# Zero products at the start on TensorE, and the mask products of an attention stage on four 64x64 tiles

## The chip, the core and the metric

The kernel runs on one core of a Trainium2 chip. The metric is device microseconds of one execution, as the median of several runs. TensorE multiplies; its results land in banks of PSUM. VectorE, ScalarE and GpSimd do the rest on data in SBUF, which has 128 partitions. SyncE issues all the transfers from and to HBM. The profile calls the engines PE (PEld for its weight loads), DVE, ACT, POOL and SP; "PEq" and the like are an engine's sequencer, which waits and issues.

## The reference, cut to what matters

Attention with a local window and block summaries, then two dense blocks. Only the attention's scores matter here:

```python
def _attn_ref(q, k, v):                       # (2, 8, 768, 64) each
    block, window = (32, 16)
    k_sum = k.reshape(B, H, nb, block, D).max(axis=3)
    scores_l = scale * np.matmul(q, k.transpose(0, 1, 3, 2))
    mask_l = np.abs(pos[:, None] - pos[None, :]) < window
    scores_s = scale * np.einsum('bhsd,bhnd->bhsn', q, k_sum) + np.log(block)
    scores_l_m = np.where(mask_l, scores_l, -1000000000.0)
    a = softmax(concatenate([scores_l_m, scores_s], axis=-1))
    return a @ concatenate([v, v_sum])
...
x = mish(attn_out @ w_in) @ w_out             # first dense block, _moe_ref
out = _moe2_ref(x, phi, w1, w2)               # softmax routing to 8 experts
```

## The kernel before

All work is cut into tasks. Each names its engine, the tasks that it needs and the buffers that it takes. `Plan.run` issues them in the order of a written table, `ORDER`, and takes buffers by another, `SLOT`; so each engine's instructions stand in a fixed order, and an engine works through them strictly one behind the other.

The tokens are taken in 12 tiles of 128, t = 0 to 11. For a tile, the scores of 8 heads lie in two banks, one for each parity r of the head, 4 heads to a bank, 120 columns to a head: 96 for the window of keys, 24 for the block summaries. The 128 tokens are two halves w of 64, and each half has its own window. A score product is a 64x64 product for one head and one half (line 419); it stands on the quarter of TensorE's array given by r (rows) and w (columns). Sixteen of them make a tile, in the order head pair, r, w.

For tiles t = 0 to 4 the mask is added by TensorE. Before the score products of a tile, mask products (line 414) fill both banks: `spread_sb` (128x128) against `mask_sb` (three patterns of 128 partitions by 120 columns). Partitions 0 to 63 of the mask hold 0 or a large negative number for the 96 window columns; partitions 64 to 66 hold the logarithm of the block size, in three pieces, for the 24 summary columns. One product of 128x128 and 480 columns fills a bank; at a tile on the edge of a sequence (t = 0) it is two, of 64 columns of weights each, since the halves differ. From t = 5 VectorE adds the mask; it takes `near` and `edge_t`, which the same kind of product makes once each (lines 384 and 393).

Around the start the work is this. SP issues in this order: the keys of batch 0 (`kb`, twice), `spread`, `masks`, the queries of tile 0, two small constants, the values (`vn`, twice), the queries of tile 1, the first half of the first weight block of `w_in` (`wi`), the queries of tile 2 (which must wait until the score products of tile 0 have read their buffer), the next two halves of `wi`, and so on. VectorE reduces the keys to block summaries (line 319), and POOL places these beside the window (line 372, `kplace`, once for each half). Then come the score products of tile 0, VectorE's row maxima (427), POOL's negation (431) and ScalarE's exponentials (441).

At the same time the weights of the first dense block are made. They arrive packed, 1 MB to a load, into three staging buffers, and each load is decoded by three instructions: ScalarE (line 487), VectorE's shift (488) and VectorE's merge (489). The merge sets the staging buffer free, and SP, which waits for that, issues the next load into it. Products of the first dense block (lines 611, and 617 to 619) follow.

Of the kernel before, what the change touches and what calls it, by code (L numbers as in the profile page):

```python
# [11 lines left out]
BF16 = mybir.dt.bfloat16  # L12
# [6 lines left out]
B, H, S, D = 2, 8, 768, 64  # L19
# [4 lines left out]
KW = 120  # L24
# [69 lines left out]
]  # L94
# [81 lines left out]
def local_summary_attention_mish_soft_moe(ctx: ExitStack, tc, qh, kh, vh, kb, vn, wi, wo, phi, w1, w2a, w2b,  # L176
# [72 lines left out]
    add = pl.add  # L249
# [19 lines left out]
    def const_fill(e):  # L269
        pool.memset(bnd, TINY)  # L270
        pool.memset(bnd[:, 0:5], TINY2)
# [808 lines left out]
```

## Time and profile before

| | us |
|---|---|
| median of 3 runs (range) | 290.82 (290.64 to 290.93) |
| the profiled execution | 289.33 |
| its span, first to last instruction | 287.5 |
| PE busy in the span | 268.0 (93%), 3144 matmuls |
| ACT, DVE, POOL busy | 207.8, 195.0, 52.2 |
[...]

The profiled execution has 1.8 us outside the span and is 1.5 us below the median of the runs. PE is busy for most of the span, but the share is a mean over stages. The chain that ended last runs through DVE, ACT and transfers up to 70 us, then for long stretches through PE, and through the transfers of the last weights from 246 to 273 us.

### The profile page before, as it was taken

The numbers are of one execution on the slowest core, as the hardware profiler recorded it, in microseconds if no ns is written. First come the engines' busy times: TensorE is split into PE (matmuls) and PEld (weight loads), VectorE is DVE, ScalarE is ACT, GpSimd is POOL, SyncE is SP. The second block draws the span as 40 slices with busy tenths as digits, with TensorE's granted clock in tenths as the row PEclk, the third lists the DMA queues.
The fourth block names the chain that finished last, engine by engine and source line by source line (L and its number), as shares of the span: only waits on it lengthen the run. The fifth ranks groups of instructions, "written<-read, shape, count | busy, mean of one in ns | idle before, by whom it ended". The sixth has DMA issues, their size and how long they took to land.

```text
span 287.5 us, 7828 instructions
## 1 busy us (share of the span) xinstructions
PE 268.0 (93%) x3144; PEld 151.4 (53%) x3144; DVE 195.0 (68%) x460; ACT 207.8 (72%) x488; POOL 52.2 (18%) x91
## 2 busy tenths in 40 slices
PE   0889879999999999999999999999999998999997
PEld 0557445555456564565556545455645743234475
DVE  2489899999999898778659667686523575002352
ACT  1297889979988879999969999899459653003232
POOL 1559225430070531001211111000000010100000
PEclk9997999999999999999999999999999999999999
DMA  7999999599999879999695677989988999999997
GB/s 253 415 358 344 358 339 365 137 335 308 317 246 315 154 107 222 205 241 223 241 192 128 76 222 141 299 157 210 325 317 313 370 388 314 412 423 421 423 346 252
DMA packets 58467, 80.58 MB, mean 280 GB/s; under 512 B 44352, under 2 KB 47936, under 8 KB 53824
## 3 DMA queue, kind: packets, MB, share of 16 engines
q1 hardware_dynamic: 58432, 80.10, 91.3%
q8 instruction: 24, 0.39, 0.5%
q14 instruction: 11, 0.09, 0.1%
HBM read 66.46 MB, written 3.15 MB: 242 GB/s over the span
## 4 chain that ended last, share of the span: by engine, by line
PE 44%; DVE 20%; DMA 16%; ACT 14%; issue 5%; POOL 1%; SPq 0%; DVEq 0%; ACTq 0%; POOLq 0%
PE bank L617 8%; PE bank L619 7%; PE bank L618 7%; DMA slot<-w2b 6%; DVE slot L489 4%; ACT slot L441 4%; DMA slot<-w2a 3%; PE bank L754 2%; ACT slot L625 2%; DMA slot<-kb 2%; DMA slot<-wi 2%; PE bank L472 2%; DVE slot L488 2%; DMA slot<-wo 2%; ACT L625 2%
## 5 line engine op out<-in xcount | busy, mean ns | idle before, releaser
L617 PE MATMUL bank<-slot,slot 128*128 128x512 f16 x176 | 66.9, 380 | 0.7 <-ACT slot L625 0.7
L618 PE MATMUL bank<-slot,slot 128*128 128x512 f16 x176 | 66.7, 379 | 0.0
L619 PE MATMUL bank<-slot,slot 128*128 128x512 f16 x176 | 66.7, 379 | 0.0
L456 POOL TENSOR_TENSOR slot<-slot,sm 128x480 f32<-128x480 f32 x19 | 22.7, 1197 | 91.7 <-DVE sm L452 25.2
L625 ACT ACTIVATE slot<-bank,scal 128x512 f32<-128x512 f32 x44 | 29.2, 687 | 9.8 <-PE bank L619 6.7
L641 DVE SCALAR_TENSOR_TENSOR slot<-slot,sc,slot 128x512 f16<-128x512 f32 x40 | 30.6, 774 | 4.3 <-ACT slot L637 4.0
L619 PEld LDWEIGHTS <-slot 128*128 128x128 f16 x176 | 17.2, 98 | 21.0 <-DVE slot L480 0.3
L255 ACT COPY slot<-bank 120x512 f32<-120x512 f32 (+5 forms) x45 | 17.7, 430 | 14.3 <-PE bank L923 8.3
L617 PEld LDWEIGHTS <-slot 128*128 128x128 f16 x176 | 17.4, 99 | 16.8 <-issue 0.6
L625 ACT ACT_TABLE_LOAD x20 | 25.7, 1283 | 0.8 <-PE bank L619 0.4
L618 PEld LDWEIGHTS <-slot 128*128 128x128 f16 x176 | 17.2, 98 | 16.6 <-issue 1.5
L441 ACT ACTIVATE slot<-slot,sm 128x120 f32<-128x120 f32 x56 | 21.3, 383 | 0.6 <-DVE sm L435 0.5
L441 ACT ACTIVATE slot<-bank,sm 128x120 f32<-128x120 f32 x40 | 13.9, 369 | 10.5 <-POOL sm L431 10.5
L257 DVE COPY slot<-bank 128x256 f32<-128x256 f32 (+3 forms) x30 | 14.4, 513 | 9.8 <-PE bank L462 4.0
L489 DVE SCALAR_TENSOR_TENSOR slot<-slot,slot 128x1024 int32<-128x1024 int32 x16 | 20.4, 1277 | 0.3
L487 ACT ACTIVATE slot<-slot 128x1024 f32<-128x1024 f32 x16 | 18.6, 1172 | 1.8 <-DMA slot<-wi 1.4
L462 PE MATMUL bank<-ident_sb,slot 128*120 128x128 f32 x96 | 14.7, 278 | 2.1 <-POOL slot L456 1.3
L360 POOL COPY slot<-slot 128x192 f32<-128x192 f32 x26 | 13.8, 550 | 12.4 <-DMA slot<-kb 12.3
L967 PE MATMUL bank<-slot,slot 128*32 128x384 f32 (+1 forms) x256 | 15.2, 382 | 0.2 <-DMA slot<-w2b 0.2
L611 PE MATMUL bank<-slot,slot 128*128 128x512 f32 x32 | 15.4, 599 | 0.0
L472 PE MATMUL bank<-slot,slot 120*64 120x64 f32 x384 | 14.6, 233 | 0.5 <-ACT phi_sb L385 0.3
L419 PE MATMUL bank<-slot,slot 64*64 64x120 f32 x384 | 14.2, 289 | 0.6 <-POOL slot L372 0.6
(175 smaller groups left out, 478.4 us busy)
## 6 DMA issues: line engine op xcount, KB each, us to landing
slot<-w SPq DMA_DIRECT2D x16, 1024.0 KB, 5.5
slot<-w2a SPq DMA_DIRECT2D x12, 960.0 KB, 9.0
slot<-wi SPq DMA_DIRECT2D x8, 1024.0 KB, 6.8
slot<-wo SPq DMA_DIRECT2D x8, 1024.0 KB, 6.0
slot<-vh SPq DMA_DIRECT2D x12, 384.0 KB, 5.3
slot<-w2b SPq DMA_DIRECT2D x4, 1024.0 KB, 18.6
slot<-kb SPq DMA_DIRECT2D x4, 768.0 KB, 5.5
slot<-qh SPq DMA_DIRECT2D x12, 256.0 KB, 5.4
```

What stands on the lines that cost most here:

```text
L255: sca.copy(dst, src)
L441: sca.activation(A_b[ha.slot][:, hp], src, AF.Exp, bias=m[:, hp:hp + 1], scale=1.0 if late else 0.125, accum_out=m[:, 4 + hp:5 + hp])
L456: (pool if e == "POOL" else vec).tensor_tensor(A_b[ha.slot], A_b[ha.slot], sm_t[hq.slot][:, 4:8].unsqueeze(2).to_broadcast([128, 4, KW]), ...
L472: pe.matmul(banks[hm.slot][64 * r:64 * r + 64, 128 * hp + 64 * w:128 * hp + 64 * w + 64], Vb[i][:, w, c:c + 64], AT_b[hat2[r].slot][0:KW, ...
L487: d = add("ACT", ("dec_a%d" % n,) + name, lambda e: sca.activation(dst(), st(1).bitcast(F32), AF.Prelu, scale=2.0 ** -112, alpha=-(2.0 ** ...
L489: return add("DVE", ("dec_o%d" % n,) + name, lambda e: vec.scalar_tensor_tensor(di(), st(0), 29, di(), op0=ALU.logical_shift_right, op1=AL ...
L611: pe.matmul(banks[hb.slot], xf_b(hx.slot)[:, dc], slots[hw.slot][:, 512 * dc:512 * dc + 512], start=(dc == 0), stop=(dc == 3))
L617: pe.matmul(ps, x[:, 0, dc], w[:, 0, dc], start=(dc == 0), stop=False)
L618: pe.matmul(ps, x[:, 0, dc], w[:, 1, dc], start=False, stop=False)
L619: pe.matmul(ps, x[:, 1, dc], w[:, 0, dc], start=False, stop=(dc == 3))
L625: g_done[t, fb] = [add("ACT", ("mish", t, fb), lambda e, dst=dst, hb=hb, sc=sc: sca.activation(dst(), banks[hb.slot], AF.Mish, scale=sc), ...
L641: d = add("DVE", ("glo", t, fb), lambda e: vec.scalar_tensor_tensor(pv(1), g(), sfb[:, t // TB:t // TB + 1], pv(0), op0=ALU.mult, op1=ALU. ...
```

## The change

The order of the tasks that both kernels have, and what each engine issues of them, is the same; the tables have other numbers because 24 tasks are put in, and some buffers of equal kind (banks, small tiles) are swapped. What is new: POOL fills `vsum` with zeros first of all; TensorE runs 22 products on these zeros, 128x128 by 480 columns, into bank 0, which nobody reads; ScalarE copies halves of `spread_sb` and `mask_sb` to the other half of the partitions when they have landed; and each mask product becomes two for each quarter of the array, 96 columns a head from the window's mask and 24 from the summaries' constant.

```diff
 ORDER = [
-    6, 7, 213, 11, 22, 189, 8, 12, 2, 192, 190, 3, 188, 191, 23, 25, 194, 195, 196, 197, 214, 0, 1, 215, 9, 10,
+    7, 8, 9, 10, 11, 12, 13, 14, 15, 16, 17, 18, 19, 20, 21, 22, 23, 24, 25, 26, 27, 28, 29, 31, 32, 2, 3, 4, 212,
...
+    def both_halves(e):
+        lo, hi = HALF
+        sca.copy(spread_sb[hi, 0:64], spread_sb[lo, 0:64])
+        sca.copy(spread_sb[lo, 64:128], spread_sb[hi, 64:128])
+        sca.copy(mask_sb[hi, :, 0:96], mask_sb[lo, :, 0:96])
+        sca.copy(mask_sb[lo, 0, 96:KW], mask_sb[hi, 0, 96:KW])
+    L_mask, L_spread = add("ACT", ("mask2",), both_halves, [L_spread, L_mask]), None
+
+    def add_mask(ps, r, w, of, stop):
+
+        a, at = ps.shape[1], (64 * r, 64 * w)
+        for stat, row, cols in ((slice(0, 64), of, slice(0, 96)), (slice(64, 128), 0, slice(96, KW))):
+            mov = mask_sb[HALF[r], row, cols]
+            pe.matmul(ps[HALF[w], :, cols], spread_sb[HALF[r], stat], mov.unsqueeze(1).to_broadcast([64, a, cols.stop - cols.start]), start=cols.start == 0, stop=stop and cols.start > 0, tile_position=at)
...
+    Z_w = add("POOL", ("fillw",), lambda e: pool.memset(vsum, 0.0))
+    hwarm = Hold(hring)
+    zeros = vsum.bitcast(BF16)
+    warm = [Z_w]
+    for j in range(22):
+        warm.append(add("PE", ("warm", j), lambda e: pe.matmul(banks[hwarm.slot][:, 0:480], zeros[:, 0:128], zeros[:, 0:480], start=True, stop=True), [warm[-1]], acq=[] if j else [hwarm], use=[hwarm] if j else []))
...
-        vc = add("ACT", ("vgather", b), gather, [vs] + old_v, use=[hb])
+        vc = add("ACT", ("vgather", b), gather, [vs] + (old_v or [warm[-1]]), use=[hb])
...
-                for rows, of in () if late else [(slice(0, 128), 1)] if kind == 1 else [(slice(0, 64), min(kind, 1)), (slice(64, 128), max(kind, 1))]:
-                    pe.matmul(ps[rows], spread_sb[:, rows], mask_sb[:, of].unsqueeze(1).to_broadcast([128, 4, KW]), start=True, stop=False)
+                for w, of in () if late else [(0, min(kind, 1)), (1, max(kind, 1))]:
+                    add_mask(ps, r, w, of, False)
```

`near_mask` and `edge_mask` call `add_mask` too, for r = 0 and both halves.

TensorE's rows at the start of the program before: the mask products of tile 0 are its first, and its score products follow.

```order
L1076 UNCONDITIONAL_BRANCH
L414 LDWEIGHTS spread_sb
L414 MATMUL bank_64<-mask_sb,spread_sb 64x480
...
L414 LDWEIGHTS spread_sb
L414 MATMUL bank_65<-mask_sb,spread_sb 64x480
L419 MATMUL bank_64<-slot_90,slot_88 64x120 x2
L419 MATMUL bank_65<-slot_90,slot_88 64x120 x2
```

The same place of the changed program, from the last of the 22 zero products on (line 292).

```order
L292 LDWEIGHTS vsum
L292 MATMUL bank_61<-vsum 128x480
L280 LDWEIGHTS spread_sb
L280 MATMUL bank_64<-mask_sb,spread_sb 64x4x96
L280 LDWEIGHTS spread_sb
L280 MATMUL bank_64<-mask_sb,spread_sb 64x4x24
...
L280 LDWEIGHTS spread_sb
L280 MATMUL bank_65<-mask_sb,spread_sb 64x4x24
L443 MATMUL bank_64<-slot_90,slot_88 64x120 x2
L443 MATMUL bank_65<-slot_90,slot_88 64x120 x2
```

The zero products stand ahead of everything, and for a tile there are eight mask products in pairs, a wide and a narrow one on each quarter of the array, before the score products (line 443 now).

ScalarE's rows at the start of the program before: after loading its table it goes straight to the exponentials of tile 0, then to the first decoding step.

```order
L1007 ACT_TABLE_LOAD
L441 ACTIVATE slot_91,sm_106<-bank_64,sm_106 128x120 x4
L395 ACTIVATE edge_t<-bank_67 128x240
L441 ACTIVATE slot_91,sm_107<-bank_65,sm_107 128x120 x4
L487 ACTIVATE slot_77<-slot_80 128x1024
L255 COPY vsum<-bank_68 24x128 x4
```

And of the changed program.

```order
L1031 ACT_TABLE_LOAD
L269 COPY spread_sb<-spread_sb 64x64
L270 COPY spread_sb<-spread_sb 64x64
L271 COPY mask_sb<-mask_sb 64x3x96
L272 COPY mask_sb<-mask_sb 64x24
L465 ACTIVATE slot_91,sm_106<-bank_64,sm_106 128x120 x4
L419 ACTIVATE edge_t<-bank_67 128x240
L465 ACTIVATE slot_91,sm_107<-bank_65,sm_107 128x120 x4
L511 ACTIVATE slot_77<-slot_80 128x1024
```

Four copies are put in between the table load and the exponentials; behind them ScalarE's order is the old one.

## Rows read from the trace of the kernel before

**Rows 1.** Chain of waits, 0 to 70 us: start us, us, what.
```profile
1.21 6.03 DMA slot<-kb
7.26 1.76 DVE slot L319
...
24.52 5.99 DMA slot<-wi
...
61.84 5.41 DMA slot<-wo
```

**Rows 2.** Timeline of PE: start us, us, engine, line, operation, shapes, count [idle before].
```profile
7.79 1.01 PE L414 MATMUL bank<-mask_sb,spread_sb 128*64 128x480 bf16 x4 [7.79 <-DMA mask_sb<-masks]
9.39 2.08 PE L419 MATMUL bank<-slot,slot 64*64 64x120 f32 x32 [0.59 <-POOL slot L372]
11.41 0.41 PE L393 MATMUL bank<-mask_sb,spread_sb 128*64 128x120 bf16 x4
11.75 2.77 PE L328 MATMUL bank<-slot,bmean_sb 128*24 128x128 f32 x48
14.45 0.58 PE L414 MATMUL bank<-mask_sb,spread_sb 128*128 128x480 bf16 x2
14.96 1.05 PE L419 MATMUL bank<-slot,slot 64*64 64x120 f32 x32
...
20.90 1.63 PE L419 MATMUL bank<-slot,slot 64*64 64x120 f32 x32
...
25.84 1.88 PE L611 MATMUL bank<-slot,slot 128*128 128x512 f32 x4
```

**Rows 3.** Windows of one us: PE, PEld, DVE, ACT, POOL busy, PEclk, DMA share, GB/s.
```profile
9.00:10.00 1.00, 0.60 (x9) 0.61 (x13) 0.01 (x1) 0.00 (x0) 0.48 (x2) 1.00 1.01 412
...
22.00:23.00 1.00, 1.00 (x22) 0.70 (x16) 0.96 (x2) 0.96 (x6) 0.88 (x1) 0.50 0.94 328
```

**Rows 4.** Timeline of ACT, 11 to 25 us.
```profile
15.13 0.40 ACT L441 ACTIVATE slot<-bank,sm 128x120 f32<-128x120 f32 x1
...
15.84 1.16 ACT L487 ACTIVATE slot<-slot 128x1024 f32<-128x1024 f32 x1 [0.22 <-DMA slot<-wi]
17.02 1.06 ACT L255 COPY vsum<-bank 24x128 f32<-24x128 f32 x4
18.11 0.59 ACT L255 COPY slot<-bank 120x512 f32<-120x512 f32 x1
...
20.41 1.18 ACT L487 ACTIVATE slot<-slot 128x1024 f32<-128x1024 f32 x1
```

**Rows 5.** Timeline of DVE, 9 to 25 us.
```profile
16.16 0.82 DVE L456 TENSOR_TENSOR slot<-slot,sm 128x480 f32<-128x480 f32 x1
16.90 0.64 DVE L427 TENSOR_REDUCE sm<-bank 128x4 f32<-128x480 f32 x1
17.58 0.17 DVE L431 TENSOR_SCALAR sm<-sm 128x4 f32<-128x4 f32 x1
17.66 0.69 DVE L488 TENSOR_SCALAR slot<-slot 128x1024 int32<-128x1024 int32 x1
...
19.71 1.31 DVE L489 SCALAR_TENSOR_TENSOR slot<-slot,slot 128x1024 int32<-128x1024 int32 x1
...
21.86 0.66 DVE L488 TENSOR_SCALAR slot<-slot 128x1024 int32<-128x1024 int32 x1
22.56 1.89 DVE L489 SCALAR_TENSOR_TENSOR slot<-slot,slot 128x1024 int32<-128x1024 int32 x1
```

**Rows 6.** Timeline of POOL, 0 to 15 us.
```profile
0.73 0.13 POOL L270 MEMSET bnd<- 128x35 f32 x1 [0.29 <-POOLq L1073]
...
5.59 0.18 POOL L343 MEMSET slot<- 128x96 f32 x1
...
9.07 0.48 POOL L372 COPY slot<-slot 128x96 f32<-128x96 f32 x2 [0.76 <-DVE slot L319]
```

**Rows 7.** Timeline of SP's issues, 7 to 12 us.
```profile
11.92 0.43 SPq L496 DMA_DIRECT2D slot<-wi  x1
```

**Rows 8.** DMA issues at 1.67, 11.92 and 21.09 us: KB each, us to landing.
```profile
spread_sb<-spread SPq DMA_DIRECT2D x1, 32.0 KB, 5.8
...
slot<-wi SPq DMA_DIRECT2D x1, 1024.0 KB, 8.4
...
slot<-wi SPq DMA_DIRECT2D x1, 1024.0 KB, 5.7
```

**Rows 9.** Windows by stage, columns as in rows 3.
```profile
2.00:15.00 13.00, 6.62 (x94) 4.37 (x94) 5.14 (x6) 2.50 (x15) 5.06 (x20) 1.00 1.00 382
...
25.00:27.00 2.00, 2.00 (x17) 1.41 (x15) 1.95 (x5) 1.91 (x4) 1.97 (x4) 1.00 0.91 250
27.00:53.00 26.00, 23.04 (x172) 12.54 (x171) 24.74 (x50) 23.26 (x49) 11.41 (x13) 1.00 0.99 346
```

More of the change, by code (lines that the diff above doesn't have):

```diff
@@ L96 @@
     "DVE": [
[4 rows of a table removed]
[4 rows of a table added]
     ],
     "POOL": [
-        196, 199, 203, 222, 229, 243, 246, 250, 253, 267, 270, 274, 277, 291, 294, 298, 301, 317, 323, 366,
-        388, 407, 413, 426, 432, 445, 451,
+        220, 223, 227, 246, 253, 267, 270, 274, 277, 291, 294, 298, 301, 315, 318, 322, 325, 341, 347, 390,
+        412, 431, 437, 450, 456, 469, 475,
     ],
@@ L383, in near_mask, with mm @@
         hm = Hold(mring)
-        q = add("PE", ("near_mm",), lambda e: pe.matmul(banks[hm.slot][:, 0:KW], spread_sb, mask_sb[:, 1], start=True, stop=True), [L_spread, L_mask] + W2_parts, acq=[hm])
+        def mm(e):
+            for w in range(2):
+                add_mask(banks[hm.slot][:, 0:KW].rearrange("p (a k) -> p a k", a=1), 0, w, 1, True)
+        q = add("PE", ("near_m4",), mm, [L_spread, L_mask] + W2_parts, acq=[hm])
         near_done.append(add("ACT", ("near_ev",), lambda e: sca.mul(near, banks[hm.slot][:, 0:KW], 0.125), [q], use=[hm]))
@@ L391, in mm @@
             for n in range(2):
-                for rows, of in ((slice(0, 64), n), (slice(64, 128), n + 1)):
-                    pe.matmul(banks[hm.slot][rows, KW * n:KW * n + KW], spread_sb[:, rows], mask_sb[:, of], start=True, stop=True)
-        q = add("PE", ("edge_mm",), mm, [L_spread, L_mask], acq=[hm])
+                for w in range(2):
+                    add_mask(banks[hm.slot][:, KW * n:KW * n + KW].rearrange("p (a k) -> p a k", a=1), 0, w, n + w, True)
+        q = add("PE", ("edge_m4",), mm, [L_spread, L_mask], acq=[hm])
         edge_done.append(add("ACT", ("edge_ev",), lambda e: sca.mul(edge_t.rearrange("p n k -> p (n k)"), banks[hm.slot][:, 0:2 * KW], 0.125), [q], use=[hm]))
@@ L419, in sc @@
                         pe.matmul(banks[hs2[r].slot][64 * w:64 * w + 64, KW * hp:KW * hp + KW], Qb[i][d, 4 * w + hp], Kb[i][d, :, 4 * w + hp], start=late, stop=(late or hp == 3), tile_position=(64 * r, 64 * w))
-        s = add("PE", ("S" + ("" if late else "m" if kind == 1 else "e"), t), sc, [lq, *lks, kp[0], kp[1], L_spread, L_mask] + [last_S[0]], acq=hs2)
+        s = add("PE", ("S" + ("" if late else "m4" if kind == 1 else "e4"), t), sc, [lq, *lks, kp[0], kp[1], L_spread, L_mask] + [last_S[0]], acq=hs2)
         last_S[0] = S_t[t] = s
```

159 rows, old and new, of tables (CHOICE, ORDER, SLOT) are left out of this document.

## The prediction

> **What bounds the kernel now.** I read the chain of waits first, from the start to 70 us, because all edits lie before 55 us but one (the product for `near`, made once). It begins with the keys: their second half lands at 7.24, VectorE reduces it, and much later it passes twice through weight loads, `wi` issued at 24.52 and `wo` at 61.84 [rows 1]. PE owns none of the long pieces there. So the question is how far the stretch between 9 and 24.5 us moves the issue at 24.52; from there on the two programs do the same work.
>
> Next I read PE alone [rows 2]. Its first products wait for the mask until 7.79, then the score products of tile 0 wait for POOL's `kplace`, start at 9.39 and take 2.08. The same 32 records take 1.05 at 14.96. [...] PE worked without a pause from 9.39, and by 14.45 its products have the short duration. Later there is a stretch at the low level that the column does show, 0.50 at 22 us [rows 3], where the scores of tile 2 take 1.63 [rows 2].
>
> Then I read what ScalarE and VectorE wait for [rows 4, 5]. ScalarE's exponentials of tile 0 end a little after 15.5, and then it idles 0.22 until the first half of `wi` lands, at 15.84. From there it has no gap up to the second decoding step at 20.41. That step's load was issued at 11.92 and took 8.4 to land, so it lands at about 20.3 [rows 7, 8]: ScalarE would not be much earlier even if it were free. VectorE starts its shift for the first half at 17.66, 0.66 after ScalarE had delivered at 17.00, because the normalization, the maxima and the negation of tiles 0 and 1 lie ahead of it. The shift for the second half starts at 21.86, 0.27 after ScalarE's 20.41 + 1.18 = 21.59. The merge behind it ends at 22.56 + 1.89 = 24.45 and lets the load at 24.52 go.
>
> Last, the transfers: their share is 1.00 between 2 and 15 us, 0.99 between 27 and 53, and 0.91 in the dip at 25 to 27 [rows 9]. Up to 53 us there is little idle transfer time to win.
>
> **The change part by part.**
>
> *Zero products.* POOL's fill of `vsum`, 512 columns, is not in the trace; fills of 35 and 96 columns take 0.13 and 0.18 [rows 6], so 0.05 for 61 columns, and 512 are about 0.5 (an estimate). The first product starts at about 1.4. One costs half of the distance that two 480-column products need at the short duration: in 14.45 to 15.03 there are two, each some 0.37 long, so 0.21 apart; at the low level 0.42. If the level rises after r, the 22 end at r + (22 - (r - 1.4)/0.42) x 0.21 = 0.5r + 5.3. Before, the rise came 5.1 us after the gapless work began (9.39 to 14.45), 6.7 after the first product (7.79). Counted from 1.4 that makes r = 6.5 to 8.1 and an end at 8.6 to 9.4. Nothing queued behind them on PE could run before 7.8 anyhow, and the scores cannot start before 9.39. So they cost nothing, if r stays under 8.1.
>
> *Copies on ScalarE.* Four copies, between the table load and 12.5 us, where ScalarE idles. Nearest rows: 24x128 takes 0.26, 120x512 takes 0.59 [rows 4]. So 64x64 is 0.25 each from 7.5 on (when `spread` has landed, 1.67 + 5.8, rows 8), the 288 columns of the masks about 0.42, the last 0.25: done at about 8.7. Bounds 8.5 and 9.0.
>
> *Mask products of tile 0.* They wait for these copies, not for the mask alone. Eight products follow; if the four quarters work at once, the columns are 4 x 96 + 4 x 24 = 480 for each quarter, 0.21 at the high level. That quarters do work at once is in the score rows: 32 records of 120 columns in 1.05 [rows 2], while four f32 records of 512 columns on the whole array take 1.88, 0.44 each [rows 2], which for 120 columns is 0.10 and for 32 in a row 3.3. So the masks are done at about 9.0 to 9.3, ahead of `kplace`, whose second half ends at 9.55 [rows 6]. Cost zero; without that cover it would be the difference.
>
> *Scores of tile 0.* The first quarter starts at 9.39, the rest at 9.6, when the second `kplace` has arrived; at the high level they end at 9.6 + 1.05 = 10.65 instead of 11.47. Maxima, negations, exponentials, normalization and POOL's window copies all move by 0.8.
>
> *What is left of these 0.8.* ScalarE has its first decoding step at 15.84 as before, since the load is the last to arrive; it only idles longer. VectorE has its queue ahead of the first shift empty 0.8 earlier, so the shift starts when ScalarE delivers, 17.00: 0.66 gained. At the second shift ScalarE delivers at 21.59 again: 0.25 gained. The merge then ends at 24.2, and the load at 24.52 is issued 0.25 earlier. Bounds: nothing, if this load still queues behind the one issued at 21.09, which lands at 26.8 [rows 8]; and 0.25 + 0.58 = 0.83, if the merge, now starting earlier than POOL's work beside it, takes 1.31 like the one at 19.71 instead of 1.89 [rows 5]. I take 0.3, near the shift, since POOL moves along and the dip in the transfers lies just where the earlier issue falls [rows 9].
>
> *Mask products of tiles 1 to 4.* Before, 14.45 to the first score at 14.96, 0.51. At best 0.25 now: 0.21 of columns and the score products right behind. These products lie under VectorE's and the transfers' part of the chain, so I count zero, 0.25 x 4 at most.
>
> *Waits.* The order of every engine is otherwise the old one, SP's and POOL's too, but for the fill ahead of POOL's first constants, over long before its first key copy at 5.3.
>
> Sum against the profiled execution: 289.33 - 0.3 = 289.0; that execution lies 1.5 below the median, so I take the difference to the median: 290.82 - 0.3 = 290.5.
>
> **The rivals.**
>
> *The transfers take all of it.* The load at 24.52 lands no earlier since it follows the one before it. For it: share 0.99 from 27 to 53. Against it: 0.91 in the dip. Time 290.8.
>
> *The whole gain passes.* The merge is shorter, and 0.8 reaches the load and all that follows. For it: 1.89 against 1.31. Against it: POOL's queue moves by the same 0.8. Time 290.0.
>
> *Slower: the clock rises late.* If the zero products stay at the low level, they end at 1.4 + 22 x 0.42 = 10.6, the scores start at about 11.0 and end at 11.0 + 1.9 = 12.9 instead of 11.47. The exponentials then end at about 17.0, 1.2 after the first load has landed; ScalarE, which had 0.22 to spare, and everything behind it move by 1.2: 292.0. For it: the only rise seen came after f32 score products and others, not after products on zeros. Against it: 480-column products are as dense as work can be. It decides from r = 9.6 on: then the zeros end at 10.1 and the scores, even short, end where they did.
>
> *The quarters don't overlap as ordered.* In `add_mask` the narrow product of a quarter follows its wide one, and the next quarter comes behind both. If products start strictly one behind the other, and one waits for its own quarter, the eight take 4 x 0.16 + 0.04 = 0.68 (0.16 for 384 columns by the 0.21 for 480), 0.2 more than before. At tile 0 they still end at about 9.4; at tiles 1 to 4 it is 0.2 each under other work, so 290.6, or 291.2 with 0.7 in the chain. Against it: the two passes of an f32 score product use the same quarter one after the other, and yet 32 records fit into 1.05.
> [...]
>
> **How the numbers follow.** A measurement of this kernel can tell about 0.2% (0.58 us) from no change. Chances: the forecast (gain 0.1 to 0.5) 0.42; transfers take it 0.17; whole gain 0.24; late clock, or a later fall of the clock at a worse place, 0.13; quarters in a row 0.04. Prediction 290.5. Range 289.8 to 291.3: it holds the whole gain, no gain, and quarters in a row, and leaves out most of the late clock. Faster by over 0.2%: the whole gain and the edge of the forecast, 0.26. Slower: the late clock and a part of the quarters, with something for swapped buffers, 0.17. Within: 0.57.
>
> **What would show it.** Right: the zero products turn from 0.42 to 0.21 apart before 8.1; the scores of tile 0 take about 1.2 from 9.39; ScalarE's first decoding step still waits for the load at 15.84, and its second still starts at 20.4; the shift at 17.0 and 21.6, and the next load issued at 24.2 to 24.3. The eight mask products take 0.2 to 0.3. Wrong: the loads of `wi` land earlier or later than 15.8 and 20.3, scores of tile 0 that start after 9.6, or a stretch at the low level in another place than 21 to 25 us.

## The result, and the profile after

The changed kernel takes 294.22 us (median of 4 runs, 293.24 to 294.89) beside 290.88 of the kernel before (4 runs): the ratio is 1.0136, 95% interval 1.0097 to 1.0176. It is slower by 3.3 us, where I had forecast no change that can be measured, and outside my range. All ratios here are those of the record, and they and the averages below leave out runs that lie over 1.5% above the fastest of their kernel; the two medians alone give 1.0115. The profiled execution took 293.86, 0.4 below its median; that of before lies 1.5 below its own, so of the 4.5 us between the two profiles about 3.3 are to be explained.

At the start everything went as forecast. The timeline of TensorE after (start, time taken, line, what, count, and in brackets the idle time before and its releaser):

```profile
1.31 7.56 PE L292 MATMUL bank<-vsum 128*128 128x480 bf16 x22 [1.31 <-POOL bnd L285]
8.80 0.41 PE L280 MATMUL bank<-mask_sb,spread_sb 64*64 64x384 bf16 x8
9.45 1.15 PE L443 MATMUL bank<-slot,slot 64*64 64x120 f32 x29 [0.24 <-POOL slot L393]
...
10.42 0.28 PE L443 MATMUL bank<-slot,slot 64*64 64x120 f32 x3
...
13.48 0.41 PE L280 MATMUL bank<-mask_sb,spread_sb 64*64 64x384 bf16 x8
13.79 1.05 PE L443 MATMUL bank<-slot,slot 64*64 64x120 f32 x32
...
20.12 0.65 PE L486 MATMUL bank<-ident_sb,slot 128*120 128x128 f32 x4 [3.18 <-ACT slot L256]
```

The zero products are over before 9, the mask products take 0.41, the 32 score records of tile 0 take 1.25 (9.45 to 10.70) instead of 2.08 [rows 2], and the scores of tile 1 are done 1.2 earlier. But then, in the last row, TensorE stands idle for 3.18, because ScalarE is late. The timeline of ScalarE after shows why:

```profile
8.51 0.21 ACT L272 COPY mask_sb<-mask_sb 64x24 bf16<-64x24 bf16 x1
11.73 0.36 ACT L465 ACTIVATE slot<-bank,sm 128x120 f32<-128x120 f32 x1 [3.02 <-POOL sm L455]
...
17.26 1.12 ACT L511 ACTIVATE slot<-slot 128x1024 f32<-128x1024 f32 x1 [2.42 <-DMA slot<-wi]
...
21.79 1.20 ACT L511 ACTIVATE slot<-slot 128x1024 f32<-128x1024 f32 x1
```

The copies end at 8.72 and the exponentials are early, but the first decoding step starts at 17.26 instead of 15.84 [rows 4]: the wait for the first half of `wi` has grown from 0.22 to 2.42. That load was issued at 7.67, nearly as before (7.62). The view of the transfers after, first of the stretch in which the load is issued (last figure: us to landing), then of 14 to 16 us by queue (packets, MB, share of 16 engines):

```profile
slot<-wi SPq DMA_DIRECT2D x1, 1024.0 KB, 9.6
...
q1 hardware_dynamic: 218, 0.81, 101.7%
q8 instruction: 1, 0.02, 3.4%
```

And of before, from 14 to 16 us:

```profile
q1 hardware_dynamic: 231, 0.84, 105.7%
```

The load takes 9.6 instead of 8.2 (15.81 less 7.62). And there is one packet that isn't data: 16 KB on the queue that the view calls instruction, 3.4% of 16 engines for 2 us, which is 1.07 us of one of them. It starts at 14.92. Before, the first such packet starts at 17.84, behind the landing. Each load leaves sixteen completion marks in the trace, which I take to be one for each of the 16 transfer engines that the profile counts. Those of the first `wi` load (us):

```
            first   fifteenth   sixteenth
before      15.18   15.77       15.81
after       15.00   15.83       17.23
```

So fifteen marks are where they were, and one is 1.4 late. The transfers as a whole are no slower: up to 22 us they have moved 7.56 MB before and 7.58 after.

From there the 1.4 goes on through VectorE, shift, merge, shift, merge:

```profile
18.41 0.69 DVE L512 TENSOR_SCALAR slot<-slot 128x1024 int32<-128x1024 int32 x1 [1.44 <-ACT slot L511]
...
20.52 1.31 DVE L513 SCALAR_TENSOR_TENSOR slot<-slot,slot 128x1024 int32<-128x1024 int32 x1
...
23.02 1.46 DVE L512 TENSOR_SCALAR slot<-slot 128x1024 int32<-128x1024 int32 x1 [0.25 <-ACT slot L511]
24.50 1.25 DVE L513 SCALAR_TENSOR_TENSOR slot<-slot,slot 128x1024 int32<-128x1024 int32 x1
```

The second merge ends at 25.75 instead of 24.45 [rows 5], and the next load is issued at 25.82 instead of 24.52 [rows 1]. One more thing has changed, the granted clock, on average 0.982 in this profile and 0.994 in that of before (windows after: length, busy time and count of each engine, then PEclk, DMA share, GB/s):

```profile
21.00:25.00 4.00, 3.50 (x56) 2.93 (x58) 3.61 (x9) 3.35 (x14) 3.37 (x4) 0.50 0.86 281
25.00:27.70 2.70, 2.70 (x38) 2.58 (x35) 2.27 (x5) 1.53 (x2) 2.31 (x5) 0.50 0.74 237
28.00:41.00 13.00, 10.38 (x82) 5.36 (x79) 12.43 (x26) 11.71 (x26) 4.36 (x4) 1.00 0.93 325
41.50:44.80 3.30, 3.30 (x40) 3.01 (x38) 3.27 (x5) 0.90 (x3) 0.59 (x1) 0.50 1.02 382
```

After the idle time of 3.18 TensorE is at the low level, a granted clock of 0.50, from 20.9 to 27.8, twice as long as before (21.2 to 24.6), and once more from 41.4 to 44.8. The chain of waits after now runs over TensorE there, where before it ran over VectorE and the loads:

```profile
21.50 1.01 PE bank L280 x6
...
22.59 1.63 PE bank L443 x29
24.22 1.90 PE bank L496 x32
26.12 1.79 PE bank L321 x16
...
41.75 1.91 PE bank L496 x32
```

So there are two suspects for the 3.3 us: the late load, and the clock.

### The profile page after: what moved, and what is told of

It reads as the page before. It is cut to its first block, busy times and chain, and to the rows that moved or that the text cites. A ratio compares the mean times of both kernels' runs of the same rounds, so it can differ in the third digit from the quotient of the medians.

```text
span 292.0 us, 7946 instructions
## 1 busy us (share of the span) xinstructions
PE 274.4 (94%) x3201; PEld 155.7 (53%) x3201; DVE 196.1 (67%) x460; ACT 208.9 (72%) x492; POOL 51.1 (18%) x92
## 4 chain that ended last, share of the span: by engine, by line
PE 62%; ACT 13%; DVE 12%; DMA 7%; issue 4%; POOL 0%; SPq 0%; DVEq 0%; ACTq 0%; POOLq 0%
PE bank L641 8%; PE bank L643 8%; PE bank L642 8%; PE bank L991 5%; PE bank L939 5%; DMA slot<-wi 3%; PE bank L496 3%; ACT slot L465 3%; PE bank L635 3%; PE bank L486 2%; PE bank L778 2%; DMA slot<-wo 2%; DMA slot<-kb 2%; DVE slot L513 2%; ACT slot L649 2%
## 5 line engine op out<-in xcount | busy, mean ns | idle before, releaser
L641 PEld LDWEIGHTS <-slot 128*128 128x128 f16 x176 | 17.4, 99 | 16.9 <-issue 0.6
L486 PEld LDWEIGHTS bank<-ident_sb,slot 128*120 128x120 f32 x96 | 11.3, 141 | 9.3 <-ACT slot L256 3.4
L496 PE MATMUL bank<-slot,slot 120*64 120x64 f32 x384 | 15.5, 240 | 0.5 <-DVE slot L258 0.3
L496 PEld LDWEIGHTS bank<-slot,slot 120*64 120x64 f32 x384 | 13.7, 152 | 3.1 <-issue 1.4
L381 POOL COPY slot<-slot 128x192 f32<-128x192 f32 x26 | 12.9, 519 | 12.0 <-DMA slot<-kb 12.0
```

What stands on the lines that cost most here:

```text
L486: pe.transpose(banks[ht.slot][0:KW, 128 * hp:128 * hp + 128], A_b[ha.slot][:, hp], ident_sb)
L496: pe.matmul(banks[hm.slot][64 * r:64 * r + 64, 128 * hp + 64 * w:128 * hp + 64 * w + 64], Vb[i][:, w, c:c + 64], AT_b[hat2[r].slot][0:KW, ...
L641: pe.matmul(ps, x[:, 0, dc], w[:, 0, dc], start=(dc == 0), stop=False)
```

## The experiments

Four theories. **1**: a refill of TensorE's instructions (so I call the packet of 16 KB; the trace says instruction, and that they are TensorE's is my assumption), moved forward because the change adds instructions to TensorE, takes one engine from the first `wi` load. **2**: the clock alone. **3**: the load is late because SP issues the transfers behind it 0.8 earlier. **4**: the new mask products themselves. For theory 1, I count TensorE's records (weight loads and products) ahead of its first transposes, at about 15 us: 244 before (8 + 64 + 8 + 96 + 4 + 64 for masks, scores, edge masks, means of V, masks, scores) and 316 after (44 of the zero products, and 16 instead of 8, 8 and 4). Ratios are to the kernel before on the same chip. All kernels here are made from the changed one: those with the mask products of before keep its order table and its swapped buffers, and all but e2 and e11 keep POOL's fill.

**e1 and e2, one half of the change each.** e1 has the mask products of before, e2 no zero products.

```diff
# e1
-                for w, of in () if late else [(0, min(kind, 1)), (1, max(kind, 1))]:
-                    add_mask(ps, r, w, of, False)
+                for rows, of in () if late else ...:
+                    pe.matmul(ps[rows], spread_sb[:, rows], mask_sb[:, of]..., start=True, stop=False)
# e2
-        warm.append(add("PE", ("warm", j), lambda e: pe.matmul(...
+        warm.append(add("PE", ("warm", j), lambda e: None, ...
```

> Zero products kept, mask products and their data as before (no copies on ScalarE). Theory 1 (a refill of TensorE's instructions): the two traces have the first 16 KB transfer of the instruction queue when TensorE has some 310 to 320 records behind it (307 before, at 17.84; 323 after, at 14.92). Here 44 records are added instead of 72 ahead of the first transposes, so it falls about at 15.4 to 15.9, just at the end of the first wi load: landing 15.8 to 17.0. Theory 2 (TensorE's clock alone: the scores of tile 0 end 0.6 earlier, TensorE stands idle longer and works longer at the low level): slower than before by 2 to 3.5 with the load at 15.8. Theory 3 (the wi load is late because the transfers behind it are issued 0.8 earlier): load at 17.2, slower by 3. Theory 4 (new mask products): no slower than before.

> New mask products and ScalarE's copies kept, no zero products. Theory 1: 28 more records ahead of the first transposes; the refill comes at about 17.0 to 17.3, after the first wi load has landed at 15.8: time as before, 290.3 to 291.3. Theory 2: scores of tile 0 at the old place, so the clock as before: as before as well. Theory 3: as before. Theory 4: slower, 293 or more.

e1: 1.0033 (0.9994 to 1.0071). e2: 1.0039 (1.0004 to 1.0075). Neither half costs what the whole does (e2's interval lies just above 1), so theory 4 falls, and the two halves only act together. In e2 the refill starts at 17.64 and the load lands at 15.72, as theory 1 has it. In e1 the refill starts at 17.69, not at 15.4 to 15.9: here I missed. Its load lands at 16.59, but for another reason: two of the sixteen marks are 0.95 late already in the load of `vn` ahead of it, which ends at 13.46 instead of 12.65, before any refill. In the trace of e1, two packets of 6 KB, the size of those of `vn`, took 1.48 and 1.22 us at 7.93 and 8.04, where the median is 0.23; what held them it doesn't tell.

**e3, the same work in fewer records.**

```diff
-    pe.matmul(banks[hwarm.slot][:, 0:480], zeros[:, 0:128], zeros[:, 0:480], ...)   # 22 times, bf16
+    pe.matmul(banks[hwarm.slot][:, 0:480], vsum[:, 0:128], vsum[:, 0:480], ...)     # 5 times, f32; masks as in e1
```

> Old mask products; the 22 bf16 zero products are replaced by 5 in f32, 128x128 by 480 columns too, which keep TensorE busy about as long (each some 1.6 us at the low level) with 20 records instead of 44. The scores of tile 0 then end about 0.6 earlier than before, and the transfers behind the first wi load are issued as early as in the changed kernel. Theory 1: the refill falls at 16.3 to 16.7, behind the landing of the first wi load, which is at 15.8 again: 290.0 to 291.0, no slower than before. Theory 2: load at 15.8, but slower by 2 to 3.5. Theory 3: load at 17.2, slower by about 3.

1.0014 (0.9975 to 1.0053). ScalarE's first decoding step, and a window, of e3:

```profile
15.74 1.15 ACT L508 ACTIVATE slot<-slot 128x1024 f32<-128x1024 f32 x1 [1.06 <-DMA slot<-wi]
```

```profile
22.00:24.00 2.00, 2.00 (x42) 1.70 (x36) 1.97 (x2) 0.92 (x6) 2.00 (x3) 0.50 1.00 406
```

The second `wi` load is issued at 10.98 (11.14 in the changed kernel, 11.92 before [rows 7]), and yet the first lands at 15.72: theory 3 falls. The refill came at 17.10, later than I had expected. TensorE is at the low level from 19.7 to 26.5, as long as after, though not again at 41, and the kernel is not measurably slower: by itself this long low stretch doesn't make the 3.3 us either. The 5 products in f32 are 10 records of products and keep TensorE busy nearly as long as the 22:

```profile
1.31 6.61 PE L292 MATMUL bank<-vsum 128*128 128x480 f32 x10 [1.31 <-POOL vsum L287]
```

**e4, records without work.** The kernel before with 72 tiny products ahead of everything.

```diff
+    pe.matmul(banks[hwarm.slot][0:32, 0:1], zeros[:, 0:32], zeros[:, 0:1], ...)   # 72 times
```

> The kernel before with 72 tiny products at its start (32 columns of weights, one column moved, on zeros) that end before the mask arrives: 144 more records for TensorE, little work, the scores of tile 0 at their old place or nearly. Theory 1: the refill falls at 14.0 to 14.9, and the first wi load lands at 16.9 to 17.3 instead of 15.8; slower by 1 to 3.5 (1.1 to 1.4 from the load, more if the clock falls for longer). Theories 2 and 3: load at 15.8, time as before.

1.0120 (1.0048 to 1.0191). From the timeline of TensorE in e4, and its transfers from 14 to 16 us and at the issue of the load:

```profile
1.31 2.08 PE L292 MATMUL bank<-vsum 128*32 128x1 bf16 x72 [1.31 <-POOL bnd L285]
7.70 1.01 PE L435 MATMUL bank<-mask_sb,spread_sb 128*64 128x480 bf16 x4 [4.31 <-DMA mask_sb<-masks]
9.34 1.88 PE L440 MATMUL bank<-slot,slot 64*64 64x120 f32 x29 [0.63 <-POOL slot L393]
```

```profile
q1 hardware_dynamic: 217, 0.79, 99.4%
q8 instruction: 1, 0.02, 3.5%
...
slot<-wi SPq DMA_DIRECT2D x1, 1024.0 KB, 9.6
```

The tiny products are over at 3.4, the masks and scores of tile 0 are where they were before, at the long durations (1.01 and 1.88), and TensorE idles 4.31 in between. Nothing on the way to the load is touched; but the refill starts at 14.53, the load takes 9.6 and lands at 17.15, and the kernel is as slow as the changed one. This is theory 1 by itself. In this profile VectorE's second to fourth merges end 1.2 late, as behind the late load; from the fifth on it is 2.8, since the load issued at 25.74 lands at 33.37, its last mark 2.7 behind the fifteenth. Why that one is so late isn't on record.

**e12, fewer of them,** the control to e4:

```diff
+    pe.matmul(banks[hwarm.slot][0:32, 0:1], zeros[:, 0:32], zeros[:, 0:1], ...)   # 22 times
```

> The kernel before with 22 tiny products at its start instead of 72: 44 more records, as many as the 22 zero products have, 288 ahead of the first transposes. Theory 1: the count of records moves the refill, and 288 are too few (with 288 and 292 records it fell at 17.0 to 17.7): refill behind 16.5, load at 15.8, time as before within 0.3%. Rival (any products on zeros at the start, or POOL's fill ahead of them, delay the load): load at 17, slower by 1%.

1.0013 (0.9978 to 1.0049). From 16.8 to 18.3 us, and at the issue of the load, the transfers of e12 have:

```profile
q8 instruction: 1, 0.02, 4.6%
...
slot<-wi SPq DMA_DIRECT2D x1, 1024.0 KB, 8.2
```

So it is the number of records that counts here (144 more move the refill to 14.53, 44 more to 17.41), not the products on zeros as such.

**e5 and e8, the changed kernel with the clock held, and once more as it is.** e5 has three f32 products on the identity in TensorE's idle time at 16.9.

```diff
+    pe.matmul(banks[hkeep.slot], ident_sb, ident_sb.unsqueeze(1).to_broadcast([128, 4, 128]), ...)   # 3 times, ahead of the transposes of tile 0's second half
```

> The changed kernel with three more products, f32, 128x128 by 512 columns on the identity, into a bank that nobody reads, between the Gram products of V and the transposes that wait for ScalarE; they fill 2.6 of the 3.2 us in which TensorE stands idle from 16.94 on. Theory 1: the 16 KB refill still falls at 14.9 and the first wi load still lands at 17.2, since nothing ahead of it changes; slower than the kernel before by 2 or more. Theory 2: TensorE does not fall to the low level between 20 and 28; by it alone all of the 3.3 us are given back (290.5 to 291); as a share beside theory 1, 0.5 to 1 of them (293 to 293.7).

> The changed kernel itself once more, on the chip of these runs, for a second profile. Theory 1: the refill falls at 14.8 to 15.1 again and the first wi load lands at 17.0 to 17.4; 293 to 295. If the refill's place or the late landing were chance, the load lands at 15.8 and the time is below 292.

e5: 1.0092 (1.0049 to 1.0135). e8: 1.0103 (1.0061 to 1.0146), refill at 14.83, load at 17.14: not chance. e5's filling products and a window:

```profile
16.66 2.79 PE L1032 MATMUL bank<-ident_sb 128*128 128x512 f32 x6
```

```profile
22.00:24.00 2.00, 2.00 (x64) 1.84 (x65) 1.65 (x7) 2.00 (x8) 1.38 (x3) 1.00 0.80 209
```

The same window of e8 has 0.50. With the low stretch at 20 to 28 gone (one of 3.4 us comes at 35.2), most of the loss stays; the load still lands at 17.23.

**e6 and e10, e3 with two such products.** Both are the same kernel.

```diff
     # 5 f32 zero products and old masks, as in e3
+    pe.matmul(banks[hkeep.slot], ident_sb, ident_sb.unsqueeze(1).to_broadcast([128, 4, 128]), ...)   # 2 times
```

> The variant with 5 f32 zero products and old mask products, and two of the filling products at the same place. Without them the load landed at 15.72, the scores of tile 0 were early, but TensorE ran at the low level from 19.66 for 6.8 us, and the time was that of the kernel before. Theory 2 (the long low stretch takes what the early scores gave): with the idle time filled no long low stretch, 289.3 to 290.5, faster than before by 0.3 to 1.5. Rival (the early scores gain nothing, since the loads land where they did): 290.5 to 291.3 whatever the clock does.

> The variant with 5 f32 zero products, two filling products and old mask products once more, in five rounds: its three rounds left open whether it is faster than before (0.9986, 0.9955 to 1.0016). If the 0.8 us of the early scores come through, 0.9965 to 0.999; if only a part of the clock does, 0.999 to 1.001.

0.9986 (0.9955 to 1.0016) and 1.0008 (0.9972 to 1.0044). In both the load lands at 15.7; e6's record of the clock has no low level at all (mean granted clock 1.00), e10's none from 4.3 to 287.6. From SP's timeline of e6, the load that was issued at 24.52 before:

```profile
24.32 0.33 SPq L517 DMA_DIRECT2D slot<-wi  x1
```

That is 0.20 earlier. It doesn't show in the time. What leads up to it in e6, ScalarE's second decoding step, then VectorE's shift and merge:

```profile
21.09 1.15 ACT L508 ACTIVATE slot<-slot 128x1024 f32<-128x1024 f32 x1 [0.70 <-DMA slot<-wi]
...
22.28 0.69 DVE L509 TENSOR_SCALAR slot<-slot 128x1024 int32<-128x1024 int32 x1 [1.04 <-ACT slot L508]
23.00 1.25 DVE L510 SCALAR_TENSOR_TENSOR slot<-slot,slot 128x1024 int32<-128x1024 int32 x1
```

**e7 and e9, the whole change, mended.** e7 has 5 f32 zero products (292 records) in place of 22, with the new masks; e9 the two filling products too.

```diff
-    pe.matmul(banks[hwarm.slot][:, 0:480], zeros[:, 0:128], zeros[:, 0:480], ...)   # 22 times, bf16
+    pe.matmul(banks[hwarm.slot][:, 0:480], vsum[:, 0:128], vsum[:, 0:480], ...)     # 5 times, f32
+    pe.matmul(banks[hkeep.slot], ident_sb, ...)                                     # e9 alone: 2 times
```

> The whole change, but with 5 f32 zero products (20 records) in place of 22 in bf16 (44). Records of TensorE ahead of the first transposes: 292, against 316 in the changed kernel and 388 with the 72 tiny products (both with the refill at 14.5 to 14.9) and 244 to 288 in the others (refill at 17.1 to 17.8). Theory 1: refill behind 15.8, first wi load at 15.7, 290.5 to 291.7, which is at most 0.3% slower than before. Rival (mask products and zero products together cost it, by themselves): 293.5 or more with the load at 15.7.

> The whole change with both suspects taken away: 5 f32 zero products (20 records) in place of 22 in bf16, and two filling products in TensorE's idle time after the Gram products of V. Theories 1 and 2 together: refill behind 16.5, first wi load at 15.7, no low level between 19.7 and 26.5; 289.8 to 291.0, no slower than before (with one of the two left it was +0.5% with the long low stretch, +0.9% with the late load). If the new mask products or ScalarE's copies cost something of their own, 291.5 or more.

e7: 1.0050 (1.0015 to 1.0084), more than the 0.3% that I had allowed; refill at 17.02, load at 15.75, the low level from 19.7 to 26.5 and from 40.2 to 43.6. e9: 1.0017 (0.9981 to 1.0052), refill at 17.59, the low level only from 39.9 to 43.3; its load lands at 16.41 since one of the sixteen marks is 0.57 late from `vn` on, as two were in e1. With both suspects gone the change costs nothing that can be measured, though it gains nothing.

**e11, one filling product in the kernel before.**

```diff
+    pe.matmul(banks[hkeep.slot], ident_sb, ident_sb.unsqueeze(1).to_broadcast([128, 4, 128]), ...)   # once
```

> The kernel before with one filling product (f32, 128x128 by 512) in the idle time of 0.8 us after the Gram products of V, and nothing else but swapped buffers. If a gain of the variant with zero products and fillers is the clock's (before, the low level from 21.21 to 24.63 covers the scores of tile 2), this one shows it too: 0.996 to 0.999. If it comes from the early scores of tile 0, this one is at 0.9985 to 1.0015.

0.9989 (0.9956 to 1.0021): inconclusive between the two. In the profiled execution, 290.99, the low level is at 40.5 to 43.9 instead of 21.2 to 24.6; five of the twelve runs have a mean clock of 1.00, so it isn't there in each.

All fourteen profiles together:

```
records ahead            first      first wi
of the transposes        refill     load lands    ratio
244  before              17.84      15.81         1
244  e11                 18.01      15.95         0.9989
264  e3, e6, e10         16.9-17.1  15.7          1.0014, 0.9986, 1.0008
272  e2                  17.64      15.72         1.0039
288  e12                 17.41      15.68         1.0013
288  e1 (vn late)        17.69      16.59         1.0033
292  e7                  17.02      15.75         1.0050
292  e9 (vn late)        17.59      16.41         1.0017
316  changed, e8         14.8-14.9  17.1-17.2     1.0136, 1.0103
316  e5                  14.61      17.23         1.0092
388  e4                  14.53      17.15         1.0120
```

One more thing fits in all of them. In the eight with the refill behind the first landing and `vn` in time (before, e2, e3, e6, e7, e10, e11, e12), the second `wi` load has one mark 1.2 to 2.1 us behind its fifteenth; so in these too one mark of the load beside the refill is late. In the changed kernel, whose refill comes earlier, that second load still has one 2.05 behind (19.36 and 21.41).

## Why the prediction was wrong

*Zero products, Copies on ScalarE, Mask products of tile 0, Scores of tile 0*: right. 8.9, 8.72, 0.41 for the eight, and the scores over at about 10.7, against 8.6 to 9.4, about 8.7, 0.21 and 10.65; only the eight took twice what I had written, under cover. The rivals of the late clock and of quarters that don't overlap are out: the zero products start 0.40 apart up to 6.88 and 0.20 apart from 7.29, where the trace's record of the clock begins (at 7.28, with 1.00); the four wide mask products start at 8.80 to 8.82 and the four narrow ones at 8.98 to 9.00, though the program lists each narrow one behind its wide one, so here the starts do not strictly follow the program; and from masks to scores it takes 0.31 at tile 1 instead of 0.51.

*What is left of these 0.8* is the step that failed, in its first sentence: "ScalarE has its first decoding step at 15.84 as before, since the load is the last to arrive". That the load is the last to arrive is right; that it arrives at the same time is not. I had counted the 22 products at nothing because no work waits behind them on TensorE, and left out what instructions can cost elsewhere: the profile has packets of instructions among the transfers of the sixteen engines (24 of 16 KB on q8 before, 25 after), and the share of these engines I had myself read as 1.00 between 2 and 15 us [rows 9]. 72 more records moved the refill from 17.84 to 14.92, in front of the landing of the one load that the chain waits for. Before, it falls behind this landing. The second `wi` load is late beside it there (the fifteenth mark at 19.20, the last at 20.36), but ScalarE is busy until 20.41 anyway [rows 4].

On TensorE itself the trace shows no more than a gap of 0.10 where the packet starts at 14.92 (scores to 14.84, transposes from 14.94); it is the load beside it that lands 1.4 later.

Where the refill is out of the way of the first load, the step's number comes out: e3, e6, e7 and e10 issue the next load at 24.34, 24.32, 24.36 and 24.31, against the 24.2 to 24.3 that I had written, and the first shift starts at 16.9, where I had 17.0. The rest of the working doesn't hold, so that the number agrees is in part luck. In e6, e7 and e10 it is the second load that is now late, with the refill beside it (21.06 or 21.07); ScalarE's second decoding step waits 0.6 to 0.7 for it and starts at 21.1 instead of 20.4, the shift at 22.3 instead of 21.6, and the merge makes up for it by taking 1.25, not 1.89. In e3 the shift starts at 21.59 but takes 1.40. The gain of 0.2 is too small to be measured.

How much of the 3.3 us is whose: late load against the same kernel without it, e8 less e7 is 0.5%, e5 less e9 0.75%, e4 less e12 1.1%, so 1.5 to 3.1 us. The long low level: e7 less e9 0.33%, e8 less e5 0.1%, e3 less the mean of e6 and e10 0.2%, always of one sign and always inside the intervals.

The traces say more of the clock. VectorE's eighth merge starts 3.36 or 3.37 us behind the seventh in the eight profiles that have the high level there, and 4.14 to 5.31 in the six that have the low level somewhere between 39.9 and 44.8 (changed, e2, e7, e9, e11, e12). Before, and e11:

```profile
41.53 1.22 DVE L489 SCALAR_TENSOR_TENSOR slot<-slot,slot 128x1024 int32<-128x1024 int32 x1
44.90 1.21 DVE L489 SCALAR_TENSOR_TENSOR slot<-slot,slot 128x1024 int32<-128x1024 int32 x1
```

```profile
41.22 1.23 DVE L510 SCALAR_TENSOR_TENSOR slot<-slot,slot 128x1024 int32<-128x1024 int32 x1
...
46.47 1.34 DVE L510 SCALAR_TENSOR_TENSOR slot<-slot,slot 128x1024 int32<-128x1024 int32 x1
```

And the time goes with the clock within one program: the runs of the kernel before took 290.1 us on average at a mean granted clock of 1.00 (27 runs), 290.6 at 0.994 (31) and 291.6 at 0.988 (22). The changed kernel had 0.982 or 0.983 in its four runs, and 0.982 or 0.988 in e8. At 1.00, with the load late, e5 took 292.2 (3 runs) and e4 293.1 (1), so 2.2 to 3.0 over the kernel before at the same clock. So the late load is shown as the main cause. That a low stretch can cost 0.8 to 2.0 us is shown too, at that place; its share of the 3.3 us is an estimate, 0.3 to 1.0 us by the ratios and perhaps more by the clocks of the runs. A fall of the clock at a worse place stood in my chances, without a price.

*Mask products of tiles 1 to 4* at zero and *Waits* at none: nothing speaks against them.

What stays open: what sets the time of a refill (it came with 300 to 351 records behind it, and e1 with 288 ahead of the transposes had it as late as before), and why the load lost 1.4 when the packet took 1.07. That packet and late mark were on one engine isn't on record; it is argued from fifteen marks in time and one late in the changed kernel, e4, e5 and e8, and from none being so late at that load where the refill came later (e1 and e9 have marks 1.0 and 0.6 late there, from `vn` on).

## What to carry to other kernels

Instructions that cost their own engine nothing can cost time elsewhere: here 72 more records of TensorE moved a packet of instructions from 17.84 to 14.92, and the load that the chain waits for landed at 17.23 instead of 15.81. Where the transfers are full (a share of 1.00 here) and the chain waits for one load, look in the trace for the instruction queue's packets, and see whether added instructions move one in front of that load. To have TensorE at the short duration by the scores (tile 0's take 1.25 in e3 as in the changed kernel, 2.08 before), few products that each take longer were safer here than many short ones: with the new masks, 5 in f32 (20 records, e7) gave 1.0050, 22 in bf16 (44 records, e8) 1.0103. And when a load "is the last to arrive anyhow", ask what else will be on its engines by then. One profile shows one place of the low clock level; read the granted clock of every run before you put a difference down to it.

## What the runs showed of the hardware

The first `wi` load of the changed kernel has its fifteenth mark at 15.83 and its sixteenth at 17.23, and ScalarE, which waits for it, starts at 17.26: with one packet of 16 KB and 1.07 us beside it, this load of 1 MB landed 1.4 later than before, while up to 22 us all sixteen engines moved 7.58 MB instead of 7.56. The low level of the clock comes at another place in another execution, also of the same program: at 20.9 to 27.8 and 41.4 to 44.8 in the changed kernel's profile, at 19.0 to 25.8 and 36.0 to 39.4 in that of e8; and the mean clock of the kernel before was 1.00, 0.994 or 0.988, run by run. So a median can't be put down to the place that one profile shows. 72 products of one column with 32 columns of weights take 2.08 us, 0.03 each.
